# Blocks of 512 tokens across the first two batch entries of a fused attention and MLP kernel, with some ELU values kept in DRAM

## The chip, the cores and the metric

The kernel runs on one core of one Trainium2 chip. The metric is the device time of one execution in microseconds; three runs of the kernel before gave 1104.92, 1105.22 and 1105.52 us, so its median is 1105.22 us. All times of engines and transfers below come from one further execution that the hardware profiler recorded.

## What is computed

Three stages follow each other. Eight batch entries (B = 8) of 576 tokens (S) and 8 heads pass a two-step attention through 32 packed queries; their outputs, 4608 tokens of 512 features, pass an ELU layer of width 2048 and then a softmax-gated, normalised layer of width 1024.

```python
def _attn_ref(q, k, v, p):                 # per entry and head
    p_packed = sm_attn(p, k, v)            # 32 packed rows attend to 576 tokens
    out = sm_attn(q, p_packed, p_packed)   # 576 tokens attend to the 32 rows
    ...
x = attn_out.transpose(0, 2, 1, 3).reshape(4608, 512)
h = x @ w_in                               # 512 -> 2048
g = np.where(h > 0, h, np.exp(np.minimum(h, 0)) - 1)
x2 = g @ w_out                             # 2048 -> 512
h2 = x2 @ w_in2                            # 512 -> 1024
solu = h2 * softmax(h2)
out = ((solu - mean) / sqrt(var + 1e-6) * g_ln) @ w_out2
```

## The kernel before

Precision is kept by splitting each factor of a product into a high and a low part; `mm3` (lines 65 to 69) then issues three matmuls where one would do, on lines 67, 68 and 69. The first matrix product is folded: `m_mm` multiplies the packed rows with `w_in` into `M`, and `ffn_h` multiplies `M` with the attention weights `AT`. The width of 2048 is cut into 16 feature tiles (f = 0 to 15) of 128. For each entry b, each half of 288 tokens (HS) and each f, `ffn_h` issues six matmuls of 288 columns into a PSUM tile `h`; ScalarE (ACT) and VectorE (DVE) turn it into ELU values and split them into a tile `g`; then twelve matmuls per f multiply `w_out` (a 128x128 block each) with `g` and accumulate into a pair of PSUM tiles `acc`.

How many columns those twelve matmuls have differs between two regimes.

- **Entries 0 and 1** go by steps of one half and one f (`step_nodes`, `ffn_x2`), 288 columns each, in runs of four f: f 0 to 3 for the four halves, then f 4 to 7, and so on. Each run ends in `x2_out`, which writes two tiles of 288 KB to `x2_dram`. The first run stores (SyncE's queue, SP); the other three add to what lies there, by a DMA with `accum_op` that GpSimd (POOL) issues on line 531.
- **Entries 2 to 7** go by blocks of 512 tokens (`wide_nodes`, `wide_x2`), which cross the borders of entries: of each entry's ELU values the last few columns (`REST`) go to DRAM (`rest_out`) and come back before the next entry's (`rest_in`), in a tile `E` with two buffers, which `e_take` puts into the slot `M3`. A last block (b = 8) of 384 tokens is all rest. All 16 f accumulate in PSUM, and the result is stored once.

Weights arrive as 64-bit words and are converted by `narrow` (two ACT instructions, then one DVE instruction on line 115). Their raw form waits in free slots or, where no slot is given, in the tag `stage` with two buffers.

The order on PE, DVE, ACT and SP is planned when the kernel is built. `node(...)` declares each piece of work with an engine, an estimated time, what it needs, what it takes and frees, and a due time; `order()` then simulates the engines and writes each engine's instructions in the order that comes out. An engine runs its list strictly in that order on the chip. For a DMA on SP the planner counts a transfer time (`size`); for an accumulating DMA on POOL it counts `size` 0. Up to 62 us it fills planned gaps on PE with matmuls into a spare tile (lines 1255 and 1257).

After the last block the third stage runs over 36 tiles of 128 tokens, to the end.

Of the kernel before, what the change touches and what calls it, by code (L numbers as in the profile page):

```python
# [9 lines left out]
F32 = mybir.dt.float32  # L10
# [4 lines left out]
ALU = mybir.AluOpType  # L15
# [8 lines left out]
P = 128  # L24
# [10 lines left out]
def attention_mlp_kernel(ctx: ExitStack, tc: tile.TileContext, q, k, v, v_tail, p,  # L35
# [22 lines left out]
    WIDE_T0 = 2 * S  # L58
    REST = {b: (b - 1) * (S - BLK) for b in range(1, B)}
# [11 lines left out]
    def acc_ps(name):  # L71
        return ps.tile([P, 2, 512], F32, tag="acc", name=name, bufs=2)
# [295 lines left out]
    def pp_scale(b, r):  # L368

        if r == 0:  # L370
            t = work.tile([P, HS], F32, tag="fe", name="pps0", bufs=2) if b == 0 else \
                work.tile([P, S], F32, tag="xo", name="pps1", bufs=3)
            st["pps"] = t[:, 0:2 * D].rearrange("p (r d) -> p r d", r=2)
        act.activation(st["pps"][:, r], st["pp"][:, r, 0:D], AF.Copy, scale=st["f"][:, 0, r:r + 1])
# [104 lines left out]
    def ffn_exp(b, half, f):  # L479
        o = gt[b, half, f]  # L480
        e = work.tile([P, HS], F32, tag="fe", name=f"fe{b}_{half}_{f}", bufs=2)

        act.activation(e, o[:, 0:HS], AF.Relu, scale=-1.0)
        act.activation(e, e, AF.Exp, scale=-1.0)
        gt[b, half, f] = o, e

    def ffn_max(b, half, f):
        o, e = gt[b, half, f]
        dve.scalar_tensor_tensor(out=e, in0=e, scalar=-1.0, in1=o[:, 0:HS], op0=ALU.add, op1=ALU.max)  # L489
        gt[b, half, f] = e  # L490

    def ffn_split(b, half, f):
        g = work.tile([P, 2, BLK], F32R, tag="g", name=f"g{b}_{half}_{f}", bufs=4)
        ghi, glo = g[:, 0, 0:HS], g[:, 1, 0:HS]
        e = gt[b, half, f]
        act.copy(ghi, e)
        gt[b, half, f] = ghi, glo
        yield
        dve.tensor_tensor(out=glo, in0=e, in1=ghi.bitcast(F32), op=ALU.subtract)
        yield  # L500

    def x2_tile(name):
        return work.tile([P, 2, HS], F32, tag="xo", name=name, bufs=3)

    def x2_at(b, half, i):
        t0 = b * S + half * HS
        return x2_dram[:, 2 * i:2 * i + 2, t0:t0 + HS]

    def ffn_x2(b, half, f, first, final):

        if first:
            accs[b, half] = [acc_ps(f"acc{b}_{half}_{f}_{i}") for i in range(2)]
        acc = accs[b, half]
        ghi, glo = gt.pop((b, half, f))
# [6 lines left out]
    def x2_out(b, half, f, i, again):  # L521

        o, scale = accs[b, half][i][:, :, 0:HS], WSCALE * WSCALE
        x = x2_tile(f"x2_{b}_{half}_{f}_{i}")
# [5 lines left out]
        if again:  # L530
            nc.gpsimd.dma_start(out=x2_at(b, half, i), in_=x, accum_op=ALU.add)
        else:
            sp.dma_start(out=x2_at(b, half, i), in_=x)
        yield
# [35 lines left out]
    def wide_x2(b, f, i, n):  # L570

        if f == 0:
            accs[b, i] = acc_ps(f"acc{b}_{i}")
        g = gt[b, f]
        w = wo[f // 2]
        for e in (2 * i, 2 * i + 1):
            es = slice((f % 2) * DM + e * P, (f % 2) * DM + (e + 1) * P)
            mm3(accs[b, i][:, e % 2, 0:n], (w[:, 0, es], w[:, 1, es]), g, f == 0, f == NF - 1)

    def wide_tag(b, e):  # L580
        return "at" if b >= B - 1 and e >= 2 else "xo"

    def wide_out(b, e, n):
        o, scale = accs[b, e // 2][:, e % 2, 0:n], WSCALE * WSCALE
        x = work.tile([P, 2 * HS], F32, tag=wide_tag(b, e), name=f"x2w{b}_{e}", bufs=3)[:, 0:n]
# [299 lines left out]
    def m_nodes(b, c):  # L885
        x = (b, c)
        bank, mp = ("misc", ("m", *x)), (m_slot(b, c), ("M", *x))
        node(("m", *x), PE, 1.1 if b < 2 else 1.02, [*ppt_of(b), *(("cvG", "wi", c, u) for u in range(4))],
             lambda: m_mm(b, c), takes=[bank, mp], lets=[(f"wi{c}", c)] if b == B - 1 else [],
             due=step_due(32 * b + (-5, 4, 11, 16.5)[c]) if b > 1 else None)  # L890
# [14 lines left out]
    def h_of(n):  # L905
        return ("h", *steps[n][:3]) if n < len(steps) else ("h", n // 32, n % 2, n % 32 // 2)

    def step_nodes(n):
# [5 lines left out]
        if f % 4 == 3 and half == 1:  # L914
# [29 lines left out]
    def wide_nodes(b, f):  # L944
        n = BLK if b < B else REST[B - 1]
        rest = REST[b - 1]
        due = step_due(32 * b + 2 * f) if b < B else step_due(32 * B) + TAIL_US * f
        late = 1.6 * WIDE_US
        ep, gp = ("E", (b, f)), ("g", (b, f))
        prev_x2 = ("x2w", *((b, f - 1) if f else (b - 1, NF - 1)), 1) if (b, f) > (2, 0) else ("x2", *steps[-1][:3])  # L950
# [11 lines left out]
        for half in range(2 if b < B else 0):  # L962
            x = (b, half, f)
            uses = [("AT", (b, half))] if f == NF - 1 else []
            if f % 4 == 3 and half == 1:
# [3 lines left out]
                 behind=[h_of(32 * b + 2 * f + half - 1)])  # L969
# [5 lines left out]
        if b < B:  # L975
# [3 lines left out]
              [(("gh", b, f), ACT, 0.17 + n / 1200, got, dict(takes=[gp], behind=[("gh", *((b, f - 1) if f else (b - 1, NF - 1)))] if (b, f) > (2, 0) else [])), (("gl", b, f), DVE, 0.15 + n / 960, [], dict(lets=held))])  # L979
        for i in range(2):  # L980
# [16 lines left out]
    TAIL_US = 2.2
# [43 lines left out]
    node(("e",), POOL, 0, [("cvG", "wo", 6, 1)], e_take, takes=[("M3", "E")])  # L1041
# [198 lines left out]
    ones = work.tile([P, HS], F32, tag="fe", name="ones", bufs=2)[:, 0:P]  # L1240
# [54 lines left out]
```

## Time and profile before

| what | value |
|---|---|
| median of 3 runs | 1105.22 us |
| the profiled execution's own time | 1105.46 us |
| its span in the trace | 1103.70 us |
| PE busy | 1098.7 us of the span |
| DVE, ACT busy | 829.0, 740.1 us |
| steps of entries 0 and 1 | about 31 to 211 us |
| blocks b = 2 to 8 | about 211 to 700 us |
| third stage | about 700 to 1100 us |

The span is the time between the first and the last recorded instruction; 1.76 us of the execution lie outside it. A matmul's recorded duration is longer than the distance to the next one, because matmuls are pipelined; what one costs is read from the distance of starts.

### The profile page before, as it was taken

How to read it: one execution, taken by the hardware profiler on the slowest of the kernel's cores; microseconds unless marked ns; L12 is line 12 of the kernel's file. 1: busy time of each engine (PE TensorE's matmuls, PEld its weight loads, DVE VectorE, ACT ScalarE, POOL GpSimd, SP SyncE). 2: the span in 40 equal slices, each digit the busy share in tenths (PEclk: the TensorE clock that was granted, in tenths of full speed). 3: DMA queues.
4: the chain of work that ended last, by engine and by line, in shares of the span. 5: the costliest groups of instructions: out<-in, count | busy, mean ns of one | idle time of the engine just before them, and what ended most of it. 6: DMA issues, size and time to landing. Idle time of an engine off the chain costs nothing.

```text
span 1103.7 us, 19488 instructions
## 1 busy us (share of the span) xinstructions
PE 1098.7 (100%) x7252; PEld 927.3 (84%) x7252; DVE 829.0 (75%) x1810; ACT 740.1 (67%) x1561; POOL 53.9 (5%) x66
## 2 busy tenths in 40 slices
PE   9999999999999999999999999999999999999998
PEld 7899998888888888788788889988888888888887
DVE  4977799588687688677787343588889888888775
ACT  4989966666656766757655553377777767868674
POOL 0001212100000000000000000000000000000000
PEclk9999999999999999999999999999999999999999
DMA  9937547424423533643545456411111010110001
GB/s 340 389 124 180 109 64 145 74 69 151 139 95 119 185 112 124 197 143 125 177 155 168 134 193 207 157 47 49 39 68 58 29 58 29 58 67 20 30 29 39
DMA packets 77199, 129.47 MB, mean 117 GB/s; under 512 B 11440, under 2 KB 50096, under 8 KB 75312
## 3 DMA queue, kind: packets, MB, share of 16 engines
q1 hardware_dynamic: 70576, 121.14, 33.0%
q0 software_dynamic: 6528, 7.08, 5.1%
q8 instruction: 57, 0.93, 0.4%
q14 instruction: 38, 0.31, 0.1%
HBM read 82.84 MB, written 45.35 MB: 116 GB/s over the span
## 4 chain that ended last, share of the span: by engine, by line
PE 99%; DVE 0%; issue 0%; ACT 0%
PE acc L67 13%; PE h L67 12%; PE h L68 12%; PE h L69 12%; PE acc L68 12%; PE acc L69 12%; PE o L691 12%; PE o L693 6%; PE m L396 3%; PE s L396 2%; PE spare L1257 2%; PE pp L365 1%; PE h L1255 1%; PE s L264 0%; PE pp L354 0%; PE t L326 0%
## 5 line engine op out<-in xcount | busy, mean ns | idle before, releaser
L67 PE MATMUL acc<-g,wo 128*128 128x512 f32 (+2 forms) x704 | 252.5, 359 | 0.0
L68 PE MATMUL acc<-g,wo 128*128 128x512 f32 (+2 forms) x704 | 246.8, 351 | 0.0
L69 PE MATMUL acc<-g,wo 128*128 128x512 f32 (+2 forms) x704 | 246.2, 350 | 0.0
L691 PE MATMUL o<-wo,lnT 128*128 128x512 f32 (+1 forms) x592 | 183.2, 383 | 0.0
L67 PEld LDWEIGHTS acc<-g,wo 128*128 128x128 f32 x704 | 132.0, 187 | 45.4 <-ACT E L562 15.1
L561 ACT ACTIVATE E<-h 128x288 f32<-128x288 f32 x192 | 78.7, 410 | 126.0 <-PE h L69 125.6
L489 DVE SCALAR_TENSOR_TENSOR E<-E,h 128x288 f32<-128x288 f32 x192 | 86.0, 451 | 94.8 <-ACT E L562 92.3
L67 PE MATMUL h<-AT,M 128*128 128x288 f32 x512 | 152.8, 298 | 0.3 <-DVE fe L489 0.3
L68 PE MATMUL h<-AT,M 128*128 128x288 f32 x512 | 151.5, 296 | 0.0
L69 PE MATMUL h<-AT,M 128*128 128x288 f32 x512 | 150.4, 294 | 0.0
L69 PEld LDWEIGHTS acc<-g,wo 128*128 128x128 f32 x704 | 132.2, 188 | 15.7
L68 PEld LDWEIGHTS acc<-g,wo 128*128 128x128 f32 x704 | 132.2, 188 | 11.6
L691 PEld LDWEIGHTS o<-wo,lnT 128*128 128x128 f32 x592 | 110.2, 188 | 21.8
L677 ACT COPY lnX<-lnB 32x256 f32<-32x256 f32 x284 | 114.7, 404 | 6.8 <-DVE lnB L668 2.6
L693 PE MATMUL o<-wo,lnT 128*128 128x512 f32 (+1 forms) x296 | 112.8, 383 | 0.0
L67 PE MATMUL h<-wi,x2hi 128*128 128x512 f32 x288 | 112.1, 389 | 0.0
L69 PE MATMUL h<-wi,x2hi 128*128 128x512 f32 x288 | 112.1, 389 | 0.0
L68 PE MATMUL h<-wi,x2lo 128*128 128x512 f32 x288 | 112.1, 389 | 0.0
L67 PEld LDWEIGHTS h<-AT,M 128*128 128x128 f32 x512 | 96.4, 188 | 9.3 <-issue 4.7
L68 PEld LDWEIGHTS h<-AT,M 128*128 128x128 f32 x512 | 96.1, 188 | 3.4
L69 PEld LDWEIGHTS h<-AT,M 128*128 128x128 f32 x512 | 96.1, 188 | 0.0
L631 ACT ACTIVATE e<-h,nm 128x1024 f32<-128x1024 f32 x36 | 40.2, 1117 | 81.9 <-DVE nm L626 81.9
(118 smaller groups left out, 1759.3 us busy)
## 6 DMA issues: line engine op xcount, KB each, us to landing
q<-in_q SPq DMA_DIRECT2D x16, 576.0 KB, 5.7
x2raw<-x_dram SPq DMA_DIRECT2D x9, 1024.0 KB, 5.5
out_x<-y SPq DMA_DIRECT2D x35, 256.0 KB, 2.0
raw_wi<-in_w_in SPq DMA_DIRECT2D x8, 1024.0 KB, 12.1
v<-in_v SPq DMA_DIRECT2D x16, 512.0 KB, 5.1
w_dram<-w SPq DMA_DIRECT2D x16, 512.0 KB, 3.4
k<-in_k SPq DMA_DIRECT2D x28, 288.0 KB, 4.0
x_dram<-x POOLq DMA_DIRECT2D x24, 288.0 KB, 5.9
```

The source lines that it names most:

```text
L67: pe.matmul(o, a[0], b[0], start=start, stop=False)
L68: pe.matmul(o, a[1], b[0], start=False, stop=False)
L69: pe.matmul(o, a[0], b[1], start=False, stop=stop)
L365: pe.matmul(o[h * NP:(h + 1) * NP, u1, 0:D], a_sb[0:n, c, r, u * NP:(u + 1) * NP], vv[0:n, c, d0:d0 + D], start=(c == 0), stop=(c == 4))
L396: pe.matmul(o[u * NP:(u + 1) * NP, r], w[rows, u, :], x[rows, u, :], start=True, stop=True)
L489: dve.scalar_tensor_tensor(out=e, in0=e, scalar=-1.0, in1=o[:, 0:HS], op0=ALU.add, op1=ALU.max)
L561: act.activation(e, o[:, 0:HS], AF.Relu, scale=-1.0)
L631: act.activation(e, last["o", i], AF.Exp, bias=last.pop(("nm", i)), accum_out=sm)
L677: act.copy(x, y)
L691: pe.matmul(o, t[:, x, kk], w[:, 0, cs], start=x + kk == 0, stop=x == 1 and kk == 7)
L693: pe.matmul(o, t[:, 0, kk], w[:, 1, cs], start=False, stop=False)
L1257: pe.matmul(spare[:, 0:P], ones, ones, start=True, stop=True)
```

## The change

- Entries 0 and 1 keep the steps by halves for f 0 to 3 alone (`F_RUN = 4`). Of the last half of entry 1 those steps multiply only the first 160 columns (`OWN`); the ELU values of the other 128 tokens, four tiles, go to DRAM (`rest_first`).
- For f 4 to 15 tokens 0 to 1023 are two blocks of 512 (b = 0 and 1 in `wide_nodes`), in runs of four f: (0, f 4 to 7), (1, f 4 to 7), (0, f 8 to 11), and so on. Each of these six runs ends in four accumulating DMAs of 256 KB on POOL.
- The blocks b = 2 to 8 follow, now from token 1024 on; the last one has 512 tokens, so nine blocks of 512 make up the 4608 tokens. `REST` grows by 128 columns for every entry.
- The ELU buffer of the steps becomes a constant tile `FE` of two halves, which also serves as the fourth output tile of the six runs. `E` takes the slot `M3` earlier, so the raw halves of w_out tiles 5 and 6, which lay there, now go through `stage`. Due times of `m_mm` for entries 0 and 1 and `TAIL_US` are new numbers.

```diff
-    WIDE_T0 = 2 * S
-    REST = {b: (b - 1) * (S - BLK) for b in range(1, B)}
+    REST = {b: (b + 1) * (S - BLK) for b in range(-1, B)}
+    F_RUN = 4
+    OWN = HS - REST[1]
+    FE = const.tile([P, 2, HS], F32, name="FE")
...
+    def cols_of(b, half):
+        return OWN if (b, half) == (1, 1) else HS
...
+    def rest_first(f):
+
+        sp.dma_start(out=rest_dram[0][:, f, 0:REST[1]], in_=gt["rest", f][:, OWN:HS])
...
     def wide_tag(b, e):
-        return "at" if b >= B - 1 and e >= 2 else "xo"
+        return "at" if b >= B - 1 and e >= 2 else "fe" if b < 2 and e == 3 else "xo"
...
-        t0 = WIDE_T0 + (b - 2) * BLK
-        sp.dma_start(out=x2_dram[:, e, t0:t0 + n], in_=x)
+        if b < 2:
+            nc.gpsimd.dma_start(out=x2_dram[:, e, b * BLK:b * BLK + n], in_=x, accum_op=ALU.add)
+        else:
+            sp.dma_start(out=x2_dram[:, e, b * BLK:b * BLK + n], in_=x)
...
-    runs = [(i // 2, i % 2, f0, f0 + 4) for f0 in (0, 4, 8, 12) for i in range(4)]
+    runs = [(i // 2, i % 2, 0, F_RUN) for i in range(4)]
...
+    blocks = [(b, f0, f0 + F_RUN) for f0 in range(F_RUN, NF, F_RUN) for b in range(2)]
+    blocks += [(b, 0, NF) for b in range(2, B + 1)]
...
-                       (("xout", b, e), SP, 0.4, [], dict(lets=[xo], size=0.25, behind=[("ein", B, 3)] if b == B - 1 else []))])
+                       (("xout", b, f, e), SP if b > 1 else POOL, 0.4 if b > 1 else 4, [],
+                        dict(lets=xos, size=0.25 if b > 1 else 0, behind=[("ein", B, 3)] if b == B - 1 else []))])
...
-    raws_of("wo", 5, "M3")
+    raws_of("wo", 5, None)
     raws_of("wi", 3, "wo7", "wo6")
-    raws_of("wo", 6, "M3")
+    raws_of("wo", 6, None)
     raws_of("wo", 7, None)
...
-    node(("e",), POOL, 0, [("cvG", "wo", 6, 1)], e_take, takes=[("M3", "E")])
+    node(("e",), POOL, 0, [("cvG", "wi", 1, 3)], e_take, takes=[("M3", "E")])
```

Three places of the resulting order matter later. The first is SP's queue ahead of the load of entry 2's first half of q (`q2_0`), which PE needs for the second attention step of entry 2 (`s2_2_0`). Before:

```order
L94 DMA raw_wo_6_1627<-in_w_out 128x2048
L1034 DMA g_sb_75<-in_g_ln 128x8
L241 DMA v2_0_1863<-in_v 128x1024
L242 DMA v2_0_1863<-in_v_tail 64x256
L226 DMA p_sb_80<-in_p 128x128
L247 DMA q2_0_2324<-in_q 128x1152
L247 DMA q2_1_2328<-in_q 128x1152
L231 DMA k3_1_2422<-in_k 128x2x288 x2
```

After:

```order
L564 DMA E_932<-rest1_dram_74 128x64
L567 DMA rest0_dram_73<-E_932 128x128 x2
L567 DMA rest1_dram_74<-E_932 128x64
L104 DMA raw_wo_7_0_2037<-in_w_out 128x1024
L104 DMA raw_wo_7_1_2044<-in_w_out 128x1024
L257 DMA q2_0_2055<-in_q 128x1152
L257 DMA q2_1_2058<-in_q 128x1152
L567 DMA rest1_dram_74<-E_932 128x64
```

The two halves of the raw w_out tile 7 stood some ten rows earlier before (ahead of w_in tile 3); now they stand right ahead of `q2_0`, and the queue also carries the stores and loads of the rest.

The second place is DVE ahead of its first work on `s2_2_0` (the transpose into `u2_0`). Before:

```order
L489 SCALAR_TENSOR_TENSOR fe0_0_14_2348<-fe0_0_14_2348,h0_0_14_2317 128x288
L163 TENSOR_TENSOR wo7_2330<-cv_wo7_0_2234,wo7_2330 128x512
L163 TENSOR_TENSOR wo7_2330<-cv_wo7_1_2246,wo7_2330 128x512
L499 TENSOR_TENSOR g0_0_14_2383<-fe0_0_14_2348,g0_0_14_2383 128x288
L489 SCALAR_TENSOR_TENSOR fe0_0_15_2378<-fe0_0_15_2378,h0_0_15_2355 128x288
L499 TENSOR_TENSOR g0_0_15_2404<-fe0_0_15_2378,g0_0_15_2404 128x288
L412 STREAM_TRANSPOSE u2_0_2425<-s2_2_0_2395 128x288 x2
```

After (`cv_wo6_1` is the second half of w_out tile 6 leaving `stage`; `g0_12` is block 0, f 12):

```order
L125 SCALAR_TENSOR_TENSOR cv_wo6_0_1849<-cv_wo6_0_1849,raw_wo_6_0_1576 128x512
L125 SCALAR_TENSOR_TENSOR cv_wo6_1_1862<-cv_wo6_1_1862,raw_wo_6_1_1596 128x512
L605 TENSOR_SCALAR FE_75<-acc1_8_1_1802 128x512
L173 TENSOR_TENSOR g0_12_1991<-E_932,g0_12_1991 128x512
L173 TENSOR_TENSOR wo6_2039<-cv_wo6_0_1849,wo6_2039 128x512
L173 TENSOR_TENSOR wo6_2039<-cv_wo6_1_1862,wo6_2039 128x512
L397 STREAM_TRANSPOSE ppT0_83<-pp2_1995 32x64 x8
L497 SCALAR_TENSOR_TENSOR E_932<-E_932,h0_0_13_2048 128x288
L497 SCALAR_TENSOR_TENSOR E_932<-E_932,h0_1_13_2060 128x288
L125 SCALAR_TENSOR_TENSOR cv_wo7_0_2084<-cv_wo7_0_2084,raw_wo_7_0_2037 128x512
L173 TENSOR_TENSOR g0_13_2111<-E_932,g0_13_2111 128x512
```

Before, both halves of tile 7 were long converted there; now the conversion of tile 6 and of tile 7 stands in the two feature tiles just ahead. On PE the twelve matmuls of `acc0_12` with `g0_12` and the twelve of `h0_0_14` and `h0_1_14` now stand between `g0_12` and `s2_2_0`.

The third place is POOL's queue of accumulating DMAs. Before, two close each run (entry, half, last f, output pair):

```order
L531 DMA x2_dram_72<-x2_1_0_11_0_2132 128x2x288
L531 DMA x2_dram_72<-x2_1_0_11_1_2134 128x2x288
L531 DMA x2_dram_72<-x2_1_1_11_0_2310 128x2x288
L531 DMA x2_dram_72<-x2_1_1_11_1_2308 128x2x288
L531 DMA x2_dram_72<-x2_0_0_15_0_2468 128x2x288
```

After, four close each run (block, last f, output tile):

```order
L609 DMA x2_dram_72<-x2w1_11_0_1987 128x512
L609 DMA x2_dram_72<-x2w1_11_1_1989 128x512
L609 DMA x2_dram_72<-x2w1_11_2_2042 128x512
L609 DMA x2_dram_72<-FE_75 128x512
L609 DMA x2_dram_72<-x2w0_15_0_2270 128x512
```

There are 24 of them either way, half as many groups, and the group of block 1, f 8 to 11 leaves DVE and ACT in the same rows in which the two halves of tile 7 and `q2_0` are released.

## Rows read from the trace of the kernel before

**Rows 1.** The page: busy times of PE, its clock, and the closing chain by engine

```profile
PE 1098.7 (100%) x7252; PEld 927.3 (84%) x7252; DVE 829.0 (75%) x1810; ACT 740.1 (67%) x1561; POOL 53.9 (5%) x66
PEclk9999999999999999999999999999999999999999
PE 99%; DVE 0%; issue 0%; ACT 0%
```

**Rows 2.** Busy time by window: window, length, busy us (instructions) of each engine, clock, DMA

```profile
100.00:150.00 50.00, 50.00 (x404) 47.34 (x403) 39.55 (x92) 44.02 (x99) 12.20 (x10) 1.00 0.66 124
150.00:200.00 50.00, 50.00 (x489) 45.38 (x488) 43.32 (x101) 34.01 (x77) 11.55 (x10) 1.00 0.55 97
```

**Rows 3.** Timeline of PE: start us, duration us, engine, line, form

```profile
100.41 0.30 PE L67 MATMUL acc<-g,wo 128*128 128x288 f32 x1
...
101.99 0.29 PE L67 MATMUL h<-AT,M 128*128 128x288 f32 x1
...
250.54 0.40 PE L67 MATMUL acc<-g,wo 128*128 128x512 f32 x1
...
253.30 0.29 PE L67 MATMUL h<-AT,M 128*128 128x288 f32 x1
...
275.14 0.40 PE L67 MATMUL acc<-g,wo 128*128 128x512 f32 x1
...
277.87 0.29 PE L67 MATMUL h<-AT,M 128*128 128x288 f32 x1
...
676.06 0.34 PE L69 MATMUL acc<-g,wo 128*128 128x384 f32 x1
...
678.14 0.33 PE L69 MATMUL acc<-g,wo 128*128 128x384 f32 x1
```

**Rows 4.** The closing chain in order of time: start us, us, engine, tile, line, count

```profile
1.06 5.06 PE spare L1257 x22
...
9.55 3.54 PE spare L1257 x30
13.10 1.09 PE t L326 x10
...
170.91 0.65 PE s L396 x16
```

**Rows 5.** Timeline of SP's DMA issues

```profile
83.28 0.34 SPq L94 DMA_DIRECT2D raw_wo<-in_w_out  x1
...
116.51 0.33 SPq L94 DMA_DIRECT2D raw_wo<-in_w_out  x1
116.88 0.47 SPq L1034 DMA_DIRECT2D g_sb<-in_g_ln  x1
...
165.19 0.87 SPq L247 DMA_DIRECT2D q<-in_q  x2
...
209.84 0.33 SPq L241 DMA_DIRECT2D v<-in_v  x1
...
220.60 0.33 SPq L241 DMA_DIRECT2D v<-in_v  x1
```

**Rows 6.** DMAs issued at 165.2, 209.5 to 210.2 and 220.6 us: count, size, us to landing

```profile
q<-in_q SPq DMA_DIRECT2D x1, 576.0 KB, 3.8
...
v<-in_v SPq DMA_DIRECT2D x1, 512.0 KB, 6.3
x_dram<-x POOLq DMA_DIRECT2D x1, 288.0 KB, 8.3
...
v<-in_v SPq DMA_DIRECT2D x1, 512.0 KB, 3.8
```

**Rows 7.** DMA queues from 64 to 211 us: packets, MB, share of 16 engines; the adds

```profile
q0 software_dynamic: 6116, 6.64, 36.2%
q1 hardware_dynamic: 4208, 10.07, 21.2%
...
x_dram<-x POOLq DMA_DIRECT2D x24, 288.0 KB, 5.9
```

**Rows 8.** Timeline of POOL: the adds ahead of the load of v at 209.84 us

```profile
207.70 2.44 POOL L531 DMA_DIRECT2D x_dram<-x  x2 [7.08 <-ACT x L526]
```

**Rows 9.** DVE instructions beside the places of the change: timeline, and one tile's durations

```profile
122.44 0.76 DVE L528 TENSOR_SCALAR x<-acc 128x576 f32<-128x576 f32 x1 [0.21 <-PE acc L69]
123.11 0.68 DVE L115 SCALAR_TENSOR_TENSOR wi<-cv_wi,raw_wi 128x512 uint32<-128x512 uint32 x1
...
L163 DVE TENSOR_TENSOR g<-E,g x91: 550/691/694, 274.1 to 696.9; 128x512 fp32r<-128x512 f32 x83, 128x384 fp32r<-128x384 f32 x8
```

**Rows 10.** The tile g_sb, 100 to 140 us, and the loads of E of all sizes

```profile
L187 DVE TENSOR_SCALAR g_sb<-g_sb x1: 166/166/166, 124.5 to 124.5; 128x8 f32<-128x8 f32 x1
...
DMA to landing us min/median/max: 6.5/6.5/6.5
...
E<-rest_dram SPq DMA_DIRECT2D x16, 32.0 KB, 1.8
```

**Rows 11.** Busy time by window at the end of the run, columns as in rows 2

```profile
1095.00:1100.30 5.30, 5.30 (x45) 5.13 (x43) 0.24 (x1) 0.58 (x2) 0.00 (x0) 1.00 0.22 77
1100.30:1102.95 2.65, 0.03 (x1) 0.00 (x0) 0.00 (x0) 0.37 (x1) 0.00 (x0) 1.00 0.15 49
1102.95:1103.70 0.75, 0.00 (x0) 0.00 (x0) 0.00 (x0) 0.00 (x0) 0.00 (x0) 0.51 0.00 0
```

More of the change, by code (lines that the diff above doesn't have):

```diff
@@ L370, in pp_scale @@
         if r == 0:
-            t = work.tile([P, HS], F32, tag="fe", name="pps0", bufs=2) if b == 0 else \
-                work.tile([P, S], F32, tag="xo", name="pps1", bufs=3)
+            t = fe_at() if b == 0 else work.tile([P, S], F32, tag="xo", name="pps1", bufs=3)
             st["pps"] = t[:, 0:2 * D].rearrange("p (r d) -> p r d", r=2)
@@ L480, in ffn_exp @@
         o = gt[b, half, f]
-        e = work.tile([P, HS], F32, tag="fe", name=f"fe{b}_{half}_{f}", bufs=2)
+        e = fe_at()
         act.activation(e, o[:, 0:HS], AF.Relu, scale=-1.0)
@@ L490, in ffn_max @@
         gt[b, half, f] = e
+        if (b, half) == (1, 1) and f < F_RUN:
+            gt["rest", f] = e
     def ffn_split(b, half, f):
         g = work.tile([P, 2, BLK], F32R, tag="g", name=f"g{b}_{half}_{f}", bufs=4)
-        ghi, glo = g[:, 0, 0:HS], g[:, 1, 0:HS]
-        e = gt[b, half, f]
+        n = cols_of(b, half)
+        ghi, glo = g[:, 0, 0:n], g[:, 1, 0:n]
+        e = gt[b, half, f][:, 0:n]
         act.copy(ghi, e)
@@ L529, in x2_out @@
         yield
[L530 to L533, printed above, removed]
+        sp.dma_start(out=x2_at(b, half, i), in_=x)
         yield
@@ L568, in wide_split, with wide_x2 @@
         return split(*gt[b, f], e_at(b, f)[:, 0:n])
-    def wide_x2(b, f, i, n):
-        if f == 0:
-            accs[b, i] = acc_ps(f"acc{b}_{i}")
+    def wide_x2(b, f, i, n, first, final):
+        if first:
+            accs[b, i] = acc_ps(f"acc{b}_{f}_{i}")
         g = gt[b, f]
@@ L889, in m_nodes @@
              lambda: m_mm(b, c), takes=[bank, mp], lets=[(f"wi{c}", c)] if b == B - 1 else [],
[L890 removed]
+             due=step_due(32 * b + (-5, 4, 11, 16.5)[c]) if b > 1 else step_due(16 * c + 8 * b) - 8 if c else None)
         for g in range(2):
@@ L905, in h_of @@
     def h_of(n):
-        return ("h", *steps[n][:3]) if n < len(steps) else ("h", n // 32, n % 2, n % 32 // 2)
+        if n < len(steps):
+            return ("h", *steps[n][:3])
+        b, f = wides[(n - len(steps)) // 2][:2]
+        return ("h", b, (n - len(steps)) % 2, f)
     def step_nodes(n):
@@ L926, in step_nodes @@
         j = f // 2
-        node(("x2", *x), PE, 1.6, [("gl", *x), *(("spD", "wo", j, u) for u in range(2)),
+        node(("x2", *x), PE, 1.6 if cols_of(b, half) == HS else 0.97, [("gl", *x), *(("spD", "wo", j, u) for u in range(2)),
                                    ("x2", *steps[n - 1][:3]) if n else None],
@@ L968, in wide_nodes @@
                  lambda half=half: ffn_h(b, half, f), takes=[("h", x)], lets=uses, due=due + 0.8 * half,
-                 behind=[h_of(32 * b + 2 * f + half - 1)])
+                 behind=[h_of(len(steps) + 2 * k + half - 1)])
             node(("fx", *x), ACT, 0.8, [("h", *x), ("e",)], lambda half=half: wide_exp(b, half, f), takes=hold,
@@ L978, in wide_nodes @@
         chain(lambda: wide_split(b, f, n),
-              [(("gh", b, f), ACT, 0.17 + n / 1200, got, dict(takes=[gp], behind=[("gh", *((b, f - 1) if f else (b - 1, NF - 1)))] if (b, f) > (2, 0) else [])), (("gl", b, f), DVE, 0.15 + n / 960, [], dict(lets=held))])
+              [(("gh", b, f), ACT, 0.17 + n / 1200, got, dict(takes=[gp], behind=[("gh", *prev)] if k else [])), (("gl", b, f), DVE, 0.15 + n / 960, [], dict(lets=held))])
         for i in range(2):
@@ L1239, in attention_mlp_kernel @@
     FILL_FROM, FILL_TO, FILL_PART = 0.4, 62.0, 0.8
-    ones = work.tile([P, HS], F32, tag="fe", name="ones", bufs=2)[:, 0:P]
+    ones = fe_at()[:, 0:P]
     dve.memset(ones, 1.0)
```

69 lines of the change are left out of this document (40 added, 29 removed).

## The prediction, made before the changed kernel ran

> **What bounds the kernel now.** I read the page first: PE is busy for 1098.7 of the span's 1103.7 us, the clock was granted in full in all forty slices, and the closing chain is 99% PE [rows 1]. The windows between 100 and 200 us, where the change works, say the same by themselves: PE 50.00 us of 50 twice, while DVE has 39.6 and 43.3 and ACT 44.0 and 34.0 [rows 2]. So a matmul taken away there shortens the run by its own time, DVE and ACT have 6 us and more to spare in each 50, and whatever makes PE wait lengthens the run one for one. The question is therefore how many columns PE saves and whether a load now arrives after PE asks for it.
>
> **Matmuls.** Counting the order, the `acc` matmuls before are 768 of 288 columns, 192 of 384 and 1152 of 512; after, 144 of 288, 48 of 160 and 1632 of 512. That is 288 fewer with the same sum of columns, and all others stay. The distance of starts from the first of twelve to the next piece of work prices a group [rows 3]: 288 columns 1.58 us (100.41 to 101.99), 512 columns 2.76 and 2.73 (taken 2.74), 384 columns 2.08. Before: 64 x 1.58 + 16 x 2.08 + 96 x 2.74 = 397.4 us. After: 12 x 1.58 + 136 x 2.74 = 391.6, plus 48 matmuls of 160 columns, which the trace does not show. The line through 131.7 ns (1.58/12) at 288 and 228.4 at 512 columns is 0.432 ns a column, so 77 ns at 160: 3.7 us in all and a sum of **-2.1 us**. The nearest short matmuls with a full weight block are the ten of `t` in 1.09 us and the thirty `spare` in 3.54 us [rows 4], 109 and 118 ns each although they are only 128 columns wide: they did not follow the line. At 111 ns the 48 cost 5.3 us, and the sum is **-0.5 us**. I take this one, since it is measured on matmuls of nearly that width. The ends are -2.9 (48 at 60 ns) and +0.3 (at 128 ns).
>
> The Trainium skill ("TensorE: Matmul & The Clock Gate", section "LDWEIGHTS (loading the stationary operand)") says that loading a weight block takes its columns divided by 1.2 in ns, whatever the depth; for 128 columns that is 107 ns. The rows of `t` and `spare` are near it, no run here shows a 160-column matmul of this type, and by that figure the sum would be -0.7.
>
> **DVE, ACT and the rest.** The evictions and the ELU work keep their elements; the g of a block is one instruction of 0.69 us [rows 9] where two halves took 0.45 each, so both engines get lighter: nothing on the path. SP's order has some 57 more rows, the stores and loads of the rest; each occupies SP for 0.33 us [rows 5], and SP has nothing else to do. They cost nothing except where somebody waits for a load behind them; those places follow. `m_mm` and `e_take` move without a new instruction; what they can spoil are the loads below. The last block's 128 columns more are in the sum above.
>
> **q2_0, the place that decides.** Before, the load of `q2_0` was issued at 165.19 us and PE began the `s` that reads it at 170.91 [rows 4, 5]: 5.7 us, where the load alone takes 3.8 [rows 6]. After, SP has three loads in a row: `wo7_0` and `wo7_1` of 512 KB, released by the conversions that empty `stage` (`cv_wo6_0`, `cv_wo6_1` on DVE), then `q2_0` of 576 KB. PE has the following left between `cv_wo6_1` and its `s2_2_0`: DVE's eviction into FE, about 0.70 us (between 0.68 for 512 columns and 0.76 for 576 [rows 9]); `g0_12`, 0.69; then, of PE's twelve `acc0_12`, ten at 0.228 (the first two read only the high part, which ACT writes before), and twelve of `h` at 0.132: 2.3 + 1.6 = 3.9. Together 5.3 us. From it go 0.33 for the issue of `wo7_1` ahead of `q2_0` and 0.21 for the handing over (the gap that rows 9 show behind a release): PE asks **4.8 us** after the issue of `q2_0`.
>
> When does it land? The hardware queue moved 10.07 MB in 147 us at a share of 21.2% of the sixteen engines [rows 7], 3.1 us per MB. Of the 3.8 us of `q2_0` alone, 1.6 are then transfer and 2.2 fixed. The three loads are 1.64 MB, 5.1 us, and start about 1.0 us before `q2_0` is issued (one DVE conversion and one SP issue): landing at -1.0 + 2.2 + 5.1 = 6.3 us, **1.5 us late** with nothing else under way. If 3.1 us per MB is too dear for packets of this size, this may be 0: `q` of 576 KB and `v` of 512 KB alone both took 3.8 [rows 6].
>
> Something else is under way: the block (1, f 8 to 11) closes in the same rows, and its four tiles go to POOL's adding DMAs, the fourth from FE itself. An add is dear: 24 of them took 36.2% of 147 us, 2.2 us of all sixteen engines for 288 KB [rows 7], so 2.0 for 256 KB and about 8 us for the four, wherever before it was two. What that does to a load stands in one place: `v` at 209.84 was issued when POOL had issued two adds from 207.70 on [rows 8] and landed after 6.3 us, against 3.8 for the same load at 220.60 [rows 5, 6], so two adds cost 2.5 us. Four would cost 5.0; the first two are issued earlier than `q2_0`, as POOL needs 1.2 us for each, and I let 1.9 us of them be done by then: **+3.1 us** (bounds 0 and 5.1, the loads' own time once more). Together PE waits 1.5 + 3.1 = **4.6 us** (0 to 6.6). Behind this `s` on PE everything queues; ACT stands at the same place, because the conversion of `wo7_0` comes before its next `g`. Once the load is there, DVE and ACT have slack and nothing else is late, so the loss is paid once.
>
> By the Trainium skill ("DMA: Bandwidth & Descriptors", section "Queues, rings and completion order") a DMA engine takes packets in turn from the queues for which it has work. If that holds throughout, the loads get half of each engine while adds are queued: 5.1 us more, 6.6 us late, a total near 1111.9. The 2.5 us of `v` agree in sign and are less.
>
> **Smaller waits.** `g_sb` was issued at 116.88 and landed 6.5 us later, though it has 4 KB; DVE read it at 124.53 [rows 5, 9, 10], 1.1 us after. It is now behind both raw halves of w_out tile 6 and a store, closer to its reader in DVE's order, and a waiting DVE holds up the next ELU tiles and so PE. The loads of E of 32 KB take 1.8 us [rows 10] and now fall beside adds. From 0 (hidden) to 3 us; since PE usually has a feature tile in hand, **+0.6**.
>
> **Sum.** -0.5 + 4.6 + 0.6 = +4.7. The profiled execution took 1105.46 us, 1.76 us of it outside the span, which the change does not touch: 1110.2. That execution is 0.24 above the median, so about **1110.0 us**.
>
> **Rivals.**
>
> - *The wait comes and the clock falls.* At the end of the run PE's last work starts at 1100.30; the clock is still 1.00 until 1102.95 and 0.51, the 1.2 GHz level, after it [rows 11]. So 2.6 us without work kept the clock and a longer pause lost it; 4.6 us may. At the start 22 spare matmuls took 5.06 us (230 ns each) and thirty a little later 118 ns each [rows 4]: half speed lasted between 5.1 us and the 8.5 us to 9.55. Half of that is lost, 2.5 to 4.2, about 3.4: **1113.4**.
> - *The adds are drained first or yield* (the other side). If the four tiles are evicted early and POOL has issued them before the loads, or the loads' packets are cheap, `q2_0` lands within 4.8 us of its issue, the wait is 0 to 0.4 and only the matmul saving stays: -0.5 to -2.9 with 0 to 0.6 of small waits, **1102.3 to 1105.4**, likeliest 1104. For it: the raw queue alone is only 1.5 us late by an average price. Against: the fourth add comes from FE, which is evicted behind the very conversion that frees the loads.
> - *Half of it.* The adds take turns with loads late: a wait of 1.5 to 3, small waits at 0 to 0.6: **1106 to 1108**.
> - *The change does not save what it says.* The 160-column matmuls are not bound by columns. That is my forecast's own -0.5; the other case moves every figure by 1.6.
>
> **How the numbers follow.** The wait without a fall of the clock 0.35, with it 0.20, half of it 0.20, hidden 0.25. The likeliest gives 1110.0; its own range is 1107.5 to 1112. About 0.2% is what a measurement of this kernel can tell from no change: 1103.0 to 1107.4. Faster needs the hidden case and the straight line for 160 columns: 0.14. The rest of the hidden case (0.11) and over half of the half case (0.13) are the same: 0.24. Slower: 0.62. For 8 in 10 the range takes the half case, most of the clock case and the upper part of the hidden one: 1103.3 to 1114.0, leaving out some 0.14 below and 0.05 above.
>
> **What would show it.** In the trace after: twelves of 512 columns 2.74 us apart in the steps of f 4 to 15, and twelves of 160 columns 1.33 us apart (0.9 if the line holds); a wait of PE for the load of `q`, at `s`, near 160 to 170 us, of 3 to 6 us, with `raw_wo` and `q` landing some 8 to 10 us after issue and four adds beside them; PE's busy time in the 50 us around it short by just that; the clock in the window behind it, 1.00 or 0.5; DVE waiting for `g_sb`. The prediction is wrong if PE has no wait over 1 us between 64 and 211 us; it is wrong in its cause if the wait stands before `acc` for a `g` or `wo`, not before `s` for `q`.

## The result: 11.9 us slower, and the profile after

The changed kernel takes 1117.28 us (1115.83 to 1118.21) against 1105.37 us for the kernel before beside it: a ratio of 1.0106, 95% interval 1.0089 to 1.0124. The forecast was 1110.0 with a range of 1103.3 to 1114.0. The sign was right, the size was not, and the time lies outside the range. The kernel also became uneven: its runs spread over 2.4 us, those of before over 1.1.

The profiled execution has a span of 1115.9 us, 12.2 more than before. The page answers [rows 1]: fewer matmuls, yet more busy time on PE, and one slice of forty in which the clock is not full.

```profile
PE 1101.7 (99%) x6964; PEld 908.3 (81%) x6964; DVE 823.6 (74%) x1786; ACT 731.8 (66%) x1537; POOL 46.0 (4%) x66
PEclk9999998999999999999999999999999999999999
PE 92%; DMA 3%; DVE 2%; ACT 1%; issue 1%; SPq 0%; DVEq 0%; ACTq 0%
```

The list of PE's waits over the whole span (line waited for: us in total, times, longest) says where:

```profile
PE s L405 <- DMA q<-in_q: 6.3, 2, 5.4
PE acc L79 <- DVE g L173: 1.7, 4, 0.8
```

The busy times by window (columns as in [rows 2]) give the sizes. The first two windows are those of [rows 2], where PE had 50.00 twice; the three behind them go around the long wait, and the last is 250 to 300 us.

```profile
100.00:150.00 50.00, 48.05 (x295) 37.48 (x294) 36.41 (x83) 41.99 (x89) 9.16 (x11) 1.00 0.65 134
150.00:200.00 50.00, 44.15 (x351) 33.71 (x350) 40.37 (x89) 30.86 (x65) 7.05 (x8) 0.93 0.53 123
...
168.70:174.06 5.36, 0.00 (x1) 0.04 (x2) 2.25 (x4) 4.08 (x8) 0.00 (x0) 0.84 1.06 307
174.06:179.10 5.04, 5.04 (x25) 3.35 (x26) 3.97 (x9) 2.17 (x5) 0.00 (x0) 0.50 0.53 153
179.10:185.00 5.90, 5.90 (x34) 5.17 (x34) 3.33 (x8) 2.77 (x6) 0.00 (x0) 0.99 0.05 11
...
250.00:300.00 50.00, 49.09 (x327) 40.29 (x327) 34.86 (x70) 33.19 (x73) 0.00 (x0) 1.00 0.52 164
```

PE is idle 1.95 us between 100 and 150, 5.85 between 150 and 200 (5.44 of it in one piece, as the timeline below shows) and 0.91 after 250; with 0.17 between 500 and 600 us that is 8.9 in ten waits. In the long wait the mean clock is already 0.84, and the next 5.04 us of work run at 0.50, the 1.2 GHz level: half of them, 2.5 us, is lost. Waits 8.9, clock 2.5 and the matmuls at -0.5 make 10.9 of the 12.2.

The recorded idle time is less than a wait costs, because a matmul's recorded duration reaches beyond the start of the next one. In the timeline below, the `h` at 166.76 starts 0.67 us after the `acc` at 166.09, where 0.23 is usual: 0.44 us are lost, and 0.28 are recorded as idle. Counted in this way, by the distance of starts, the ten waits cost 10.5 us. The start of the run goes the other way: with the same 682 matmuls before it, the `h` behind the wait near 62 us starts at 62.16, and in the kernel before at 62.90. So 10.5 + 2.5 - 0.5 - 0.7 = 11.8 of the 12.2 us are placed.

The place itself, timeline of PE (start us, us, engine, line, form, and in brackets the idle time before it and what ended it). Of the groups of matmuls single rows stand:

```profile
163.52 0.40 PE L77 MATMUL acc<-g,wo 128*128 128x512 f32 x1
...
166.09 0.39 PE L79 MATMUL acc<-g,wo 128*128 128x512 f32 x1
166.76 0.40 PE L77 MATMUL h<-AT,M 128*128 128x288 f32 x1 [0.28 <-DVE E L497]
...
168.32 0.29 PE L79 MATMUL h<-AT,M 128*128 128x288 f32 x1
174.06 1.22 PE L405 MATMUL s<-q,ppT 64*32 64x288 f32 x16 [5.44 <-DMA q<-in_q]
175.20 0.79 PE L77 MATMUL acc<-g,wo 128*128 128x512 f32 x1
```

SP's issues there, which answer [rows 5], and POOL's, which answer [rows 8] (start us, time of all, count):

```profile
161.31 0.92 SPq L104 DMA_DIRECT2D raw_wo<-in_w_out  x2
162.32 2.83 SPq L257 DMA_DIRECT2D q<-in_q  x2
```

```profile
160.07 1.75 POOL L609 DMA_DIRECT2D x_dram<-x2w  x2 [17.90 <-ACT x2w L603]
162.68 0.86 POOL L609 DMA_DIRECT2D x_dram<-x2w  x1 [0.85 <-ACT x2w L603]
163.22 1.21 POOL L609 DMA_DIRECT2D x_dram<-FE  x1
```

And the DMA queues while `q2_0` was on its way, 162.3 to 173.9 us, with the landing times of what was issued in it (as [rows 6, 7]):

```profile
q1 hardware_dynamic: 564, 2.11, 54.2%
q0 software_dynamic: 509, 0.94, 47.2%
...
q<-in_q SPq DMA_DIRECT2D x2, 576.0 KB, 11.6
x_dram<-x2w POOLq DMA_DIRECT2D x1, 256.0 KB, 10.2
x_dram<-FE POOLq DMA_DIRECT2D x1, 256.0 KB, 12.5
```

This is the picture of the forecast: two raw halves, then `q2_0`, and four adds beside them. The sixteen DMA engines are full (the two shares add up to 101%): the adds have 47% of them, and everything in SP's queue, almost all of it loads, 54%. `q2_0` needs 11.6 us where it took 3.8 alone [rows 6].

### The profile page after: what moved, and what is told of

The parts are those of the page before. It is cut to its first block, busy times and chain, and to the rows that moved or that the text cites. A ratio compares the mean times of both kernels' runs of the same rounds, so it can differ in the third digit from the quotient of the medians.

```text
span 1115.9 us, 19028 instructions
## 1 busy us (share of the span) xinstructions
PE 1101.7 (99%) x6964; PEld 908.3 (81%) x6964; DVE 823.6 (74%) x1786; ACT 731.8 (66%) x1537; POOL 46.0 (4%) x66
## 3 DMA queue, kind: packets, MB, share of 16 engines
q0 software_dynamic: 3456, 6.29, 3.8%
## 4 chain that ended last, share of the span: by engine, by line
PE 92%; DMA 3%; DVE 2%; ACT 1%; issue 1%; SPq 0%; DVEq 0%; ACTq 0%
PE o L709 12%; PE acc L77 12%; PE h L77 11%; PE h L78 11%; PE h L79 11%; PE acc L79 11%; PE acc L78 11%; PE o L711 6%; PE m L405 3%; PE s L405 2%; DMA q<-in_q 2%; PE spare L1284 1%; DMA E<-rest_dram 1%; PE pp L375 1%; PE h L1282 1%
## 5 line engine op out<-in xcount | busy, mean ns | idle before, releaser
L77 PE MATMUL acc<-g,wo 128*128 128x512 f32 (+2 forms) x608 | 238.0, 391 | 0.4 <-ACT g L171 0.2
L79 PE MATMUL acc<-g,wo 128*128 128x512 f32 (+2 forms) x608 | 231.6, 381 | 1.8 <-DVE g L173 1.7
L78 PE MATMUL acc<-g,wo 128*128 128x512 f32 (+2 forms) x608 | 232.0, 382 | 0.0
L573 ACT ACTIVATE E<-h 128x288 f32<-128x288 f32 x240 | 98.4, 410 | 149.4 <-PE h L79 149.1
L497 DVE SCALAR_TENSOR_TENSOR E<-E,h 128x288 f32<-128x288 f32 x240 | 106.6, 449 | 108.1 <-ACT E L574 103.6
L77 PEld LDWEIGHTS acc<-g,wo 128*128 128x128 f32 x608 | 114.6, 189 | 56.2 <-ACT E L574 21.4
L79 PEld LDWEIGHTS acc<-g,wo 128*128 128x128 f32 x608 | 114.7, 189 | 26.3 <-DVE g L173 4.2
L78 PEld LDWEIGHTS acc<-g,wo 128*128 128x128 f32 x608 | 114.7, 189 | 17.0
L574 ACT ACTIVATE E<-E 128x288 f32<-128x288 f32 x240 | 106.7, 444 | 7.6
L173 DVE TENSOR_TENSOR g<-E,g 128x512 fp32r<-128x512 f32 x128 | 87.4, 684 | 28.2 <-ACT g L171 26.5
L77 PEld LDWEIGHTS h<-AT,M 128*128 128x128 f32 x512 | 96.5, 188 | 7.1 <-DVE E L497 0.9
L78 PEld LDWEIGHTS h<-AT,M 128*128 128x128 f32 x512 | 96.1, 188 | 4.3
```

The source lines that it names most:

```text
L77: pe.matmul(o, a[0], b[0], start=start, stop=False)
L78: pe.matmul(o, a[1], b[0], start=False, stop=False)
L79: pe.matmul(o, a[0], b[1], start=False, stop=stop)
L173: dve.tensor_tensor(out=lo, in0=src, in1=hi.bitcast(F32), op=ALU.subtract)
```

## The experiments

Three readings were to be told apart. **A:** the adds take the DMA engines from the loads. **B:** three loads in one queue are enough by themselves. **C:** a second path, from the raw w_out tile 7 over ACT and DVE to g, is as long as that of q. Each run is the changed kernel with one edit; `put(order, xs, y)` moves pieces of the planned order behind `y` and leaves every other engine's order as it was.

### Adds that store (e1_stores)

```
-            nc.gpsimd.dma_start(out=x2_dram[...], in_=x, accum_op=ALU.add)
+            nc.gpsimd.dma_start(out=x2_dram[...], in_=x)
```

> The 24 DMAs of the first two blocks store instead of adding (the sum into x2_dram is left out); order, sizes and queues stay. Theory A (the adds take the DMA engines from the loads): q2_0 lands within 7 us of its issue instead of 11.6, PE's wait at s for q falls from 5.4 us to under 1, the clock stays at 1.00, DVE's wait for g_sb falls from 3.5 to under 1.5, the total is 1107 us (1105 to 1109). Rival B (three loads in one queue are enough by themselves): the wait stays at 4 us or more and the total above 1113.

Measured: 1110.12 us (1108.77 to 1112.09). In the profiled execution the clock is full in all forty slices and DVE waits 0.7 us for `g_sb` instead of 3.5; PE still waits for `q2_0`:

```profile
168.22 0.72 PE L405 MATMUL s<-q,ppT 64*32 64x288 f32 x16 [1.94 <-DMA q<-in_q]
```

From 64 to 211 us the queue of the adds, after (first) and with stores (second):

```profile
q0 software_dynamic: 2948, 5.38, 24.4%
```

```profile
q0 software_dynamic: 1920, 6.29, 11.5%
```

The second holds all 24, 0.70 us of sixteen engines each. The first holds 5.38 of their 6.29 MB; divided by 24 they are 24.4% x 147 / 24 = 1.49 us each, so an add costs at least twice a store. 7.2 us come back (5.4 against the control below), so the adds are a large part of it. But the total, the wait of 1.94 us and the landing of `q2_0`, issued at 160.0, after 8.1 us all miss what A allowed (1105 to 1109, under 1 and 7): stores of that size take engine time too, so this run cannot exclude a part for B.

### q2_0 ahead of the raw halves (e2_q_first)

```
-for x in order():
+for x in put(order(), [("raw", "wo", 7, u) for u in range(2)], ("q", 2, 0)):
```

> On SP the load of q2_0 stands ahead of the two halves of raw w_out tile 7, nothing else moves. If the wait for q is the only thing that matters there (theory A with one path): q2_0 lands by 168.5 us, the wait and the fall of the clock go, the total is 1109.5 us (1108.5 to 1111). Rival C (a second path of the same length runs from the raw tile 7 over ACT and DVE to g of block 0, f 13): the wait moves from s to the acc that reads that g, since the halves now land 2 to 3 us later, and the total is 1116 to 1119.

Measured: 1116.95 us (1116.56 to 1117.61), no gain. PE, with the idle time before and its cause:

```profile
168.53 0.72 PE L405 MATMUL s<-q,ppT 64*32 64x288 f32 x16
174.90 0.80 PE L77 MATMUL acc<-g,wo 128*128 128x512 f32 x1 [5.65 <-ACT g L171]
```

ACT at the same time:

```profile
171.56 0.66 ACT L120 ACTIVATE cv_wo<-raw_wo 128x512 f32<-128x512 f32 x1 [7.15 <-DMA raw_wo<-in_w_out]
...
173.68 0.66 ACT L120 ACTIVATE cv_wo<-raw_wo 128x512 f32<-128x512 f32 x1 [0.83 <-DMA raw_wo<-in_w_out]
174.24 0.61 ACT L171 CAST g<-E 128x512 fp32r<-128x512 f32 x1
```

The s runs almost at once, and the matmuls behind it wait 5.65 us instead, because the conversions of tile 7 stand ahead of the g of f 13 in ACT's order. The wait has only changed its name: the second path is there. That it is as long as that of q, as C says, is not shown, since the edit itself lets the raw halves land later (the second at 173.60 instead of 171.15). In the profile after, ACT wrote this g here:

```profile
171.79 0.61 ACT L171 CAST g<-E 128x512 fp32r<-128x512 f32 x1
```

With q in time PE, done with the `s` at about 169.3, would have waited for it until 172.4. That is about 3 us (an estimate from these rows) where the wait for q was 5.44. Moving one load ahead of the others does not help, since all of them are late.

### Filling the wait on PE (e4_fill, e4b_fill22)

```
-for x in order():
+for x in (y for x in order() for y in ([22, x] if x == ("s2", 2, 0) else [x])):   # 46 in e4_fill
```

> 46 spare matmuls of 128 columns (about 5 us at full clock) are put on PE ahead of the waiting s2_2_0; they only fill the wait. If the clock fell because PE had no work: the granted clock stays 1.00 through 160 to 185 us, the wait for q shrinks to under 1 us in the profile, the end comes 2.5 us earlier, 1114.8 us. If the lower clock has another cause, it stays at 0.50 behind the wait and the total is 1117.3 or more.

Measured: 1118.86 us (1118.55 to 1119.18). The clock stayed at 1.00, but the s started at 177.77, 6.2 us after its data, behind 10.43 us of filling: each spare matmul is two instructions. The test was mis-sized and says only that the clock held at 1.00 in this wait when PE had work.

> As e4_fill with 22 spare matmuls instead of 46: there each was two instructions of 0.113 us, so 46 filled 10.4 us and held the s back 6.2 us beyond the landing of q2_0; 22 fill 5.0 us, just the wait. If the fall of the clock costs 2.5 us (5.1 us of work at half rate) on top of the wait: the clock is 1.00 from 160 to 185 us, the total 2 to 3 us below the changed kernel, 1114.5 us (1113 to 1115.5). If the fall costs nothing in the end, because DVE and ACT are late there too: 1116.5 us or more.

Measured: 1112.94 us (1112.80 to 1113.35). The s comes just when `q2_0` has landed, and the clock is full in the wait and behind it:

```profile
172.54 0.72 PE L405 MATMUL s<-q,ppT 64*32 64x288 f32 x16
```

```profile
168.00:173.00 5.00, 5.00 (x58) 4.60 (x56) 2.10 (x4) 2.95 (x6) 0.00 (x0) 1.00 1.06 311
173.00:180.00 7.00, 7.00 (x46) 5.92 (x36) 5.99 (x11) 4.92 (x11) 0.00 (x0) 1.00 0.44 113
```

The total is a little below the range that was expected. Against the control below (1115.56) it is 2.6 us less with the data as late as there (`q2_0` landed at 172.06, in the control at 172.37), which agrees with the 2.5 us that 5.04 us at half rate cost. Against the 1117.28 of the first runs it would be 4.3, so the total alone fixes the cost only to within these two; the windows give the closer figure.

### Adds that wait for q2_0 (e5_adds_wait, e5b_adds_wait)

The edit in outline; in e5_adds_wait the read is a product with a constant instead of the difference:

```
+            gate = q2_0[:, 0:1] - q2_0[:, 0:1]          (GpSimd, once, ahead of the four adds)
+            x[:, 0:1] = x[:, 0:1] + gate                (e5b_adds_wait only)
             nc.gpsimd.dma_start(out=x2_dram[...], in_=x, accum_op=ALU.add)
...
+for x in put(order(), [("xout", 1, 11, e) for e in range(4)], ("q", 2, 0)):
```

> POOL reads one element of q2_0 ahead of the four adds of block 1, f 8 to 11, so that these four alone start once q2_0 has landed; all else stays. Theory A: q2_0 lands 6 to 7 us after its issue, PE's wait at s is under 1 us, the clock stays 1.00, total 1109.5 us (1108 to 1111). Rival B: the wait stays at 3 us or more, total 1114 or more. Rival C: the wait for q goes, but PE waits 2 us or more for the g of block 0, f 13 or for w_out tile 7, total 1112 to 1114.

Measured: 1115.60 us (1113.06 to 1116.79). The edit did not do what it said: POOL issued the adds at 158.5 to 161.65 and the read at 172.48, since no data tied them together. So it decides nothing; it is one more run of the changed kernel.

> In e5_adds_wait the four adds were issued before POOL's read of q2_0 and so did not wait. Here POOL first forms zero from one element of q2_0 and adds it to a column of each of the four tiles, so that the four adding DMAs of block 1, f 8 to 11 cannot start before q2_0 has landed. Theory A (these adds slow the loads): q2_0 lands 6 to 7 us after its issue, PE's wait at s is under 1 us, the clock stays 1.00, total 1109.5 us (1108 to 1111). Rival B (the three loads alone): the wait stays at 3 us or more, total 1114 or more. Rival C (the raw w_out tile 7 is late anyway): PE waits 2 us or more for the g of block 0, f 13 or f 14, total 1112 to 1114.

Measured: 1109.87 us (1108.11 to 1113.63). The landing times of `q2_0` and of the two raw halves (their median), and the s:

```profile
q<-in_q SPq DMA_DIRECT2D x1, 576.0 KB, 6.8
...
raw_wo<-in_w_out SPq DMA_DIRECT2D x2, 512.0 KB, 4.9
```

```profile
168.91 0.72 PE L405 MATMUL s<-q,ppT 64*32 64x288 f32 x16 [0.66 <-DMA q<-in_q]
```

`q2_0` lands 6.8 us after its issue, behind the same two loads; the wait is 0.66 and the clock full. B falls: with the queue alone PE waits 0.7 us, and the four adds cost 11.6 - 6.8 = 4.8 us of landing time, or 3.7 by the control below, where `q2_0` took 10.5. With the adds away the raw halves are early enough too, and the wait at g that e2_q_first showed does not appear. One of the six executions took 1113.63 us; it was not profiled, and what it waited for is open.

### g_sb early (e6_g_early)

```
-    node(("g",), SP, 0.4, [("raw", "wo", 6, 0)], ...)
+    node(("g",), SP, 0.4, [("raw", "wo", 3, 1)], ...)
```

> The load of g_sb and DVE's use of it stand some 30 us earlier, everything else as in the changed kernel. If DVE's wait of 3.5 us for g_sb reaches PE: PE's idle time between 100 and 150 us falls from 1.95 to 0.8 us and the total by 1.2 us, to 1116 us. If ACT and DVE have to wait there for the loads of E anyway, PE's idle time stays within 0.3 us of 1.95 and the total does not move.

Measured: 1114.45 us (1112.32 to 1115.36). PE's window from 100 to 150 us here, and in the control:

```profile
100.00:150.00 50.00, 49.52 (x322) 39.24 (x320) 39.19 (x88) 44.29 (x95) 9.02 (x11) 1.00 0.65 135
```

```profile
100.00:150.00 50.00, 48.49 (x303) 38.57 (x302) 37.41 (x84) 42.98 (x91) 9.68 (x11) 1.00 0.65 137
```

1.03 us of idle time are gone against the control, 1.47 against the profile after (48.05). That DVE's wait for `g_sb` cost PE about 1 us rests on this idle time: the total is 1.1 us below the control's, but the two sets of runs overlap. In the profile after DVE's wait was:

```profile
131.17 0.17 DVE L197 TENSOR_SCALAR g_sb<-g_sb 128x8 f32<-128x8 f32 x1 [3.54 <-DMA g_sb<-in_g_ln]
```

### The raw tile 7 loaded 40 us earlier (e7_wo6_slot), and both edits (e8_both)

```
-    raws_of("wo", 6, None)
     raws_of("wo", 7, None)
+    raws_of("wo", 6, "wo7")
...
-    node(("g",), SP, 0.4, [("raw", "wo", 6, 0)], ...)
+    node(("g",), SP, 0.4, [("raw", "wo", 3, 1)], ...)
...
+    last = narrow_nodes("wo", j, u, ..., needs=[("cvG", "wo", 6, 1)] if j == 7 else [])
```

> g_sb early as in e6_g_early; and the raw w_out tile 7 is loaded in place of tile 6 through the two staging buffers, tile 6 as one load of 1 MB into the slot of tile 7 some 15 us before q2_0; the adds stay as they are. So q2_0 has no load right ahead of it, but all four adds beside it. If the trouble needs both (loads in a row and adds): q2_0 lands 6 to 7 us after its issue, PE's wait is under 1 us, the clock 1.00, total 1107.5 us (1106 to 1109). If the adds alone make q2_0 late: the wait stays at 3 us or more, total 1112 or more.

Measured: 1109.08 us (1106.69 to 1110.34). The raw tile 7 is issued at 121.3 us instead of 161.3, tile 6 at 142.2. With all four adds beside it, `q2_0` landed 7.1 us after its issue and PE waited 0.59 us:

```profile
168.13 0.72 PE L405 MATMUL s<-q,ppT 64*32 64x288 f32 x16 [0.59 <-DMA q<-in_q]
```

Its landing, and the queues in these 7.1 us:

```profile
q<-in_q SPq DMA_DIRECT2D x1, 576.0 KB, 7.1
```

```profile
q0 software_dynamic: 368, 0.68, 66.7%
q1 hardware_dynamic: 187, 0.79, 34.3%
```

So A falls in its plain form too: neither the adds nor the loads ahead of it are enough alone (0.59 and 0.66 us of wait); together they are 4.4 to 5.4 us and the clock. About 1 us of what this run gains is that of `g_sb`.

> e7_wo6_slot with the waiting adds of e5b_adds_wait added: neither a load ahead of q2_0 nor an add beside it. PE's remaining 0.6 us at this s should go and the rest of e7's waits stay (about 1.2 us between 150 and 160, 0.9 and 0.8 us at two later s, 0.5 before 150): total 1108 us (1106.5 to 1109.5). If the two edits were only two ways to the same gain, it equals e7_wo6_slot within 1 us; if adds that start later spoil something behind them, it is above 1109.5.

Measured: 1108.83 us (1108.12 to 1110.20). The s no longer waits, and the total is that of e7_wo6_slot: the two edits are two ways to the same gain. The landing of `q2_0`:

```profile
q<-in_q SPq DMA_DIRECT2D x1, 576.0 KB, 4.9
```

With that the four cases stand side by side: 4.9 us with neither loads nor adds, 6.8 with the loads alone, 7.1 with the adds alone, 10.5 and 11.6 with both. Each alone adds about 2 us, the two together 5.6 to 6.7, more than their sum. PE asks 6.3 to 6.7 us after the issue in these runs, so either alone is almost hidden and only both together are not.

The PE windows of e8_both between 64 and 700 us show what is left:

```profile
64.00:150.00 86.00, 85.50 (x587) 71.55 (x580) 64.59 (x136) 72.95 (x158) 10.81 (x12) 1.00 0.57 138
150.00:160.00 10.00, 8.96 (x89) 6.45 (x77) 8.47 (x24) 7.92 (x17) 0.00 (x0) 1.00 0.04 11
160.00:170.00 10.00, 9.71 (x118) 7.69 (x108) 9.72 (x24) 8.80 (x19) 3.98 (x9) 1.00 0.47 128
170.00:250.00 80.00, 79.17 (x593) 64.34 (x592) 60.97 (x143) 49.82 (x112) 8.77 (x10) 1.00 0.58 139
250.00:700.00 450.00, 449.05 (x3108) 368.29 (x3107) 304.89 (x677) 268.35 (x595) 0.00 (x0) 1.00 0.54 174
```

3.6 us of small waits (0.50 + 1.04 + 0.29 + 0.83 + 0.95), for loads of q and for E and g, where the kernel before had none in the windows of [rows 2]. Counted by the distance of starts, as in the section on the result, they cost 5.1; with -0.5 for the matmuls and 0.3 for an earlier start (62.59 instead of 62.90) that is 4.3 where the span is 4.1 us above that of the kernel before. So they are what keeps this version above it (1108.83 against 1105.01).

### The control (e9_control)

> The changed kernel once more, unaltered, beside e8_both on one chip: 1117 us (1115.5 to 1118), PE's wait for q at s 5 us or more and the clock at 0.50 behind it in the profiled execution. If its time is 1114.5 or less, the gain read from e6_g_early (1114.45 against 1117.28 of other runs) is not one.

Measured: 1115.56 us (1114.66 to 1115.62), so the changed kernel lies between 1115.6 and 1117.3 us from one set of runs to another, and a gain of 1 to 2 us between sets cannot be told from that. The wait in this profile was 4.4 us, less than the 5 that were expected, with the clock at 0.50 behind it (172.50 to 177.29 us):

```profile
PE s L405 <- DMA q<-in_q: 4.4, 1, 4.4
```

`q2_0` landed a little sooner than in the profile after:

```profile
q<-in_q SPq DMA_DIRECT2D x1, 576.0 KB, 10.5
```

## Why the prediction was wrong in size and right in cause

Two steps failed most. The sum has no term for the clock, because "the loss is paid once": it cost 2.5 us more. And the smaller waits stand in it at 0.6 us and measured 3.4, or 4.9 by the distance of starts. The wait at `s2_2_0` itself came out 0.8 us longer in the profile after and 0.2 shorter in the control's.

- **Matmuls, -0.5: right.** Twelve of 160 columns take 1.30 us between the starts of the first of them and of the next h, 72.24 to 73.54: 108 ns each, near the 111 that was chosen from `t` and `spare` [rows 4] and far from the line's 77.

```profile
72.24 0.23 PE L77 MATMUL acc<-g,wo 128*128 128x160 f32 x1
...
73.54 0.33 PE L77 MATMUL h<-AT,M 128*128 128x288 f32 x1
```

  Over all `acc` matmuls, by the mean distance of starts where no wait falls between, e8_both, whose clock was full, comes to about 0.7 us less than the kernel before.

- **The wait at s2_2_0, 4.6 us: right in place and cause, right in size by two errors that cancel, which is luck.** It was 5.4 and 4.4 us in two profiles. The landing was taken as 6.3 + 3.1 = 9.4 us after the issue and was 11.6 and 10.5: the three loads alone took 6.8 (e5b_adds_wait), not 6.3, and the adds cost 4.8 and 3.7, not 3.1. (In the 6.3, the transfer of `q2_0` is a slip: 576 KB at 3.1 us per MB are 1.8 us, not 1.6, which would have made it 6.1.) The step that failed is the 1.9 us taken off the 5.0, scaled from `v` behind two adds [rows 6, 8], for a head start: two adds had been issued before the loads, but the second of them landed only at 170.20, the other two were issued 0.4 and 0.9 us behind `q2_0` (162.68 and 163.22), and both queues were busy to the end. On the other side PE asked 6.3 us after the issue (168.62), not 4.8: twelve h still stood ahead of `acc0_12`, which therefore began at 163.52, after its g was there, and the h behind it waited for E.

  The Trainium skill ("DMA: Bandwidth & Descriptors", section "Queues, rings and completion order") says that a DMA engine takes packets in turn from the queues for which it has work. The prediction's estimate from that, half of each engine and so 5.1 us, is above what the adds cost here. The shares in the profile after, 54% and 47%, agree with halves, those of e7_wo6_slot, 34% and 67%, do not.

- **The clock: the rival that came true.** The prediction gave the case with the clock's fall 1113.4 us and a chance of 0.20, less than the same wait without it. The rows it used leaned the other way: at the end of the run a pause of 2.6 us kept the clock and it was 0.51 behind that [rows 11], and the predicted wait of 4.6 was well beyond. Its price, 3.4 us, was set between 2.5 and 4.2; it was 2.5 by the window behind the wait and 2.6 by e4b_fill22. Together with the smaller waits this is most of the miss: here a wait of 4.4 and one of 5.4 us on PE were not paid once.

- **Smaller waits, 0.6: too small.** They were 3.4 of the 8.9 us of idle time. PE lost 1.95 us between 100 and 150 us, about 1.0 of it through `g_sb` as named; the rest in waits for a g, and 0.4 between 150 and 168 for a g and for E. And 0.9 us through the next entry's first half of q, which the prediction had not looked at. There `q` landed 6.9 us after an issue at 249.55; in the kernel before it took 5.05 and was there 1.0 us before PE asked. New beside it are a load of E of 64 KB and a rest store of 96 KB instead of 32; which of them it was has not been tried. This wait comes and goes: in the control's profile it was 0.07 us, in that of e8_both 0.83 and another 0.70 at 407.57, for a later q. "They cost nothing except where somebody waits" was the right rule, applied to two places instead of to every load that had little time to spare.

- **ACT's second path: named, and its weight missed.** "ACT stands at the same place" is what e2_q_first showed, but the prediction drew from it that the loss is paid once, not that moving the load of q would bring nothing.

- **Chances and range.** 0.62 for slower was the right side. With the measured parts in the prediction's own sum, -0.5 + 5.4 + 2.5 + 3.4 = 10.8, the forecast would have been 1116.0, between the control and the first runs. The upper end of 1114.0 lies just above the clock's case, 1113.4, which has the small waits at their chosen 0.6; with those at their own bound of 3 the same case gives 1115.8, and the range should have reached there. Even that is below the 1117.28 of the first runs.

## What to carry to other kernels

When a change puts loads behind each other, count what all queues move at the same moment, and ask of each load how much time it had to spare before, not only of those that the change names; here a load of 3.8 us took 11.6. Where PE is the bound, a wait of several microseconds is forecast and the trace before shows the clock lost behind a shorter pause, the clock's loss belongs to the likeliest case, not to a rival. And where two paths end at one place, moving one of them shows nothing until the other is moved too: e2_q_first gained nothing (0.3 us against the first runs, and it is 1.4 slower than the control). The removal of either common cause gave 5.4 to 7.4 us: e5b_adds_wait 5.7 to 7.4, and e7_wo6_slot, less the 1.1 us of `g_sb`, 5.4 to 7.1.

## What the runs showed of the hardware

The clock of TensorE fell within a pause of 5.44 us (mean 0.84 in its last 5.36) and stayed at 0.50 for 5.04 us of full work behind it; with spare matmuls in the pause it stayed at 1.00. An adding DMA of 256 KB from GpSimd's queue took at least 1.5 us of all sixteen DMA engines, and the same DMA as a store 0.70. SP's and GpSimd's queues, both busy, had 54% and 47% of the engines over the 11.6 us in the profile after, and 34% and 67% over the 7.1 us in e7_wo6_slot. A load of 576 KB landed after 4.9 us with neither loads ahead nor adds beside it, 6.8 and 7.1 with one of the two, 10.5 and 11.6 with both.
